# Turning float64 words into float32 on VectorE, with the intermediate word in a PSUM bank instead of in SBUF

## The chip, the cores and the metric

The kernel runs on one core of one Trainium2 chip. The metric is the device time of one execution in microseconds (us). A core has five engines with a queue of their own: TensorE (PE, with its weight loads as PEld), VectorE (DVE), ScalarE (ACT), GpSimd (POOL) and SyncE (SP, which issues the DMAs). Each works through its queue in order; semaphores hold an instruction back until what it needs is there. SBUF is the working memory, PSUM the eight banks into which TensorE writes.

## The reference

Three stages in a row: causal softmax attention, a gated block with a short causal convolution, and a block that mixes tokens with a sine and a cosine.

```python
# q, k, v: (4, 12, 448, 64) -> attention output x: (4, 448, 768)
scores = np.where(mask, -1e9, (1/8) * q @ k.T)
attn   = softmax(scores) @ v
# second block, weights 768 x 768, conv_w 5 x 768
gate = sigmoid(sum over t of conv_w[t] * x shifted by t)
x2   = (gate * (x @ w_val)) @ w_out
# third block, w_tok_r and w_tok_i 448 x 448
theta = x2 @ w_theta
y = w_tok_r @ (x2 * cos(theta)) + w_tok_i @ (x2 * sin(theta))
u = x2 + y
out = u + max(u @ w_ch, 0)
```

q, k and v arrive as float32. The seven weight arrays arrive as float64, so each number is two 32-bit words, a low one and a high one, and the kernel has to make float32 of them itself.

## The kernel before, in words

The first batch's attention (12 heads, one iteration of `attn_iter` each, in five pieces) runs alone; from then on `dense(b)` of one batch is interleaved with the attention of batch b+1, by the table `RATE`. `dense(b)` runs four stages of six column blocks of 128: x @ w_val with the gate (`hf`), w_out (`x2f`), theta with sine and cosine, the token mix (`ztr`, `tok`), and w_ch. Every matrix product is made with numbers that are split into a high and a low part, three matmuls for one. The tile tool, not the source, settles the final order on each engine: it reorders what the source asks for.

Conversion of weights: `load_w(n, g)` brings half a column block as 128 x 384 pairs of words into a tile `cv_raw` (48 of these; ring "wb" of 8 buffers, shared with `w_hl`). `stage_w` calls `to_f32` on it (L152 to L161), `split_w` has POOL make the high part (L104) and POOL or DVE the low part (L107, L110) in a tile `w_hl`, which L226 writes to DRAM for the later batches. `load_tok` does the same for eight 112 x 448 pieces of the token weights (`tok_bits`, into `tok_raw`), and `setup_conv` for 30 x 128 words of the convolution weights. That makes 57 calls of `to_f32`, all of them in the first 310 us of the execution.

`to_f32` has four steps, on views of the tile that take every second word: L152 (DVE) turns the low word into a number of 0 to 7; L155 (DVE) adds the sign of the high word to it; L158 (ACT) scales the high word; L159 (DVE) shifts it by three and joins both. L155 and L159 are the two with two tensor operands.

PSUM: `psum(tag)` hands out banks: two for the tag "mm" (matrix products), six for every other tag, all of them in one ring named "at". The scores `ps_s` (L320, L321, read by DVE at L322 and by ACT at L115), the transposes `ps_tr` (L283, L341, L394, L569, L610) and the attention output `ps_av` (L364, read by DVE at L424) all live in that ring of six.

Of the kernel before, what the change touches and what calls it, by code (L numbers as in the profile page):

```python
# [9 lines left out]
F32 = mybir.dt.float32  # L10
F32R = mybir.dt.float32r
I32 = mybir.dt.int32
U32 = mybir.dt.uint32
AF = mybir.ActivationFunctionType
ALU = mybir.AluOpType
# [33 lines left out]
def kernel(  # L49
# [14 lines left out]
    nc = tc.nc  # L64
# [34 lines left out]
    def psum(tag):  # L99
        at = "mm" if tag == "mm" else "at"  # L100
        return ps.tile([P, 512], F32, tag=at, name=f"ps_{tag}", bufs=2 if tag == "mm" else 6)
# [36 lines left out]
    def setup_conv():  # L138
        t = pool.tile([P, CV, 2], I32, tag="wb", name="cv_raw", bufs=8)
        nc.sync.dma_start(  # L140
            out=t[: KW * KC, 0:P, :].rearrange("p n two -> p (n two)"),
            in_=conv_w.rearrange("k (c n) -> (k c) n", n=2 * P),
        )
        c32 = pool.tile([P, S], F32, tag="tmp", name="c32")[:, 0:P]
        to_f32(c32[: KW * KC, :], t[: KW * KC, 0:P, :])
        pt = psum("tr")
        nc.tensor.transpose(pt[:, : KW * KC], c32[: KW * KC, :], ident[: KW * KC, : KW * KC])
        nc.vector.tensor_copy(cw.rearrange("p k c -> p (k c)"), pt[:, : KW * KC])

    def to_f32(dst, raw):  # L150
        hi, lo = raw[:, :, 1], raw[:, :, 0]
        nc.vector.tensor_scalar(  # L152
            out=lo, in0=lo.bitcast(U32), scalar1=2.0**-29, scalar2=7.0, op0=ALU.mult, op1=ALU.min
        )
        nc.vector.scalar_tensor_tensor(  # L155
            out=lo, in0=hi, scalar=-(2**31), in1=lo, op0=ALU.bitwise_and, op1=ALU.bitwise_or
        )
        nc.scalar.activation(hi.bitcast(F32), hi.bitcast(F32), AF.Abs, scale=2.0**-112)  # L158
        nc.vector.scalar_tensor_tensor(  # L159
            out=dst.bitcast(I32), in0=hi, scalar=3, in1=lo, op0=ALU.logical_shift_left, op1=ALU.bitwise_or  # L160
        )  # L161

    tok_raw = []
# [1 line left out]
    def load_tok(c):  # L165
        t = pool.tile([P, NZ * P], F32, tag=("zt_h", "zt_l")[c % 2], name="tok_raw")
        for a, w in enumerate((w_tok_r, w_tok_i)):
            r = pool.tile([P, S, 2], I32, tag="z", name="tok_bits", bufs=3)
            nc.sync.dma_start(
                out=r[:CP].rearrange("p n two -> p (n two)"), in_=w[c * CP : (c + 1) * CP, :]  # L170
            )
            to_f32(t[:CP, a * S : (a + 1) * S], r[:CP])
        tok_raw.append(t)
# [28 lines left out]
    def stage_w(n, g):  # L202
        if n < NW:
            to_f32(bits[n, g][:, :, 0], bits[n, g])
# [546 lines left out]
```

## Time and profile before

| | |
|---|---|
| median of 3 runs | 796.83 us (794.93 to 798.34) |
| the profiled execution, its own time | 796.42 us |
| its span, first to last instruction | 794.6 us |
| PE busy | 713.9 us (90%) |
| DVE busy | 503.7 us (63%) |
| ACT busy | 429.3 us (54%) |
| POOL busy | 314.4 us (40%) |
| TensorE's mean granted clock | 0.976 |

The shares are averages over stages that differ. The chain of waits is the chain of work that ended last, followed back from the end: what stands on it set the time, and what does not stand on it was covered by other work. A group's mean against its minimum or its median tells how much of its time was waiting inside the instruction.

### The profile page before, as it was taken

What the parts mean: (1) busy time and instruction counts of PE and PEld (TensorE: products, weight loads), DVE (VectorE), ACT (ScalarE), POOL (GpSimd) and SP (SyncE); (2) the same over time, 40 slices, a digit from 0 to 9 for tenths busy, and PEclk for the clock granted to TensorE, in tenths of its full rate; (3) what the DMA queues carried; (4) which work ended last, traced back from release to release, by engine and by line L of the source; (5) the groups of instructions that cost most, each with busy time, mean ns of one, the idle gap of its engine ahead of it and who ended that gap; (6) DMA issues with size and microseconds to landing.
All of it is one profiled execution on the core that took longest, in us unless ns stands there. A gap on an engine that the chain in (4) does not pass through costs nothing.

```text
span 794.6 us, 11969 instructions
## 1 busy us (share of the span) xinstructions
PE 713.9 (90%) x3989; PEld 603.9 (76%) x3989; DVE 503.7 (63%) x1131; ACT 429.3 (54%) x1004; POOL 314.4 (40%) x327
## 2 busy tenths in 40 slices
PE   6977897696879898999899899999899999999997
PEld 4555576575667787788788788788798797988996
DVE  4889989999997655643756644752766733115531
ACT  5888765546577643544777633544787522125401
POOL 0688795574553766332235610122133232201100
PEclk9999899899999999999989999999999999999999
DMA  9546359688765279678833159678814068774323
GB/s 234 118 118 187 104 129 323 139 256 208 222 122 144 44 232 254 184 201 216 172 78 84 43 166 210 171 188 199 178 45 103 14 144 231 216 221 128 94 67 84
DMA packets 145419, 124.63 MB, mean 157 GB/s; under 512 B 87855, under 2 KB 120397, under 8 KB 145357
## 3 DMA queue, kind: packets, MB, share of 16 engines
q1 hardware_dynamic: 145357, 123.86, 60.5%
q8 instruction: 32, 0.52, 0.3%
q14 instruction: 30, 0.25, 0.1%
HBM read 99.38 MB, written 24.44 MB: 156 GB/s over the span
## 4 chain that ended last, share of the span: by engine, by line
PE 52%; DVE 22%; DMA 9%; ACT 8%; POOL 4%; issue 3%; SPq 0%; ACTq 0%; DVEq 0%; POOLq 0%
PE ps_mm L488 28%; PE ps_mm L583 10%; DMA out_dram<-o 4%; PE ps_av L364 4%; PE ps_tr L341 3%; DVE cv_raw L155 3%; DVE ps_s L322 2%; DVE cv_raw L159 2%; PE ps_s L320 2%; DVE gate L450 2%; PE ps_s L321 2%; DVE qs L110 2%; DVE cv_raw L152 2%; ACT prob L115 2%; PE ps_tr L569 1%
## 5 line engine op out<-in xcount | busy, mean ns | idle before, releaser
L488 PE MATMUL ps_mm<-act_hi,w_hl 128*128 128x448 f32 x864 | 272.7, 377 | 15.0 <-POOL w_hl L104 5.4
L488 PEld LDWEIGHTS ps_mm<-act_hi,w_hl 128*128 128x128 f32 x864 | 164.3, 192 | 32.4 <-POOL w_hl L104 6.8
L488 PE MATMUL ps_mm<-act_lo,w_hl 128*128 128x448 f32 x432 | 159.9, 371 | 0.8 <-DVE act_lo L110 0.8
L115 ACT ACTIVATE prob<-ps_s,negm 112x112 f32<-112x112 f32 x192 | 95.1, 497 | 64.7 <-DVE negm L322 63.2
L322 DVE CUSTOM_DVE_ANT_0 ps_s<-ps_s,mask 112x112 f32<-112x112 f32 x192 | 85.6, 455 | 62.9 <-PE ps_s L321 52.0
L107 POOL TENSOR_TENSOR act_lo<-x2f,act_hi 128x448 fp32r<-128x448 f32 x36 | 43.6, 1210 | 128.6 <-ACT act_hi L502 63.0
L320 PE MATMUL ps_s<-kk,qs 128*112 128x256 f32 x192 | 71.2, 374 | 18.9 <-DVE qs L110 7.2
L488 PEld LDWEIGHTS ps_mm<-act_lo,w_hl 128*128 128x128 f32 x432 | 82.8, 192 | 6.3 <-DVE act_lo L110 1.2
L354 ACT COPY pt<-ps_tr 112x448 f32<-112x448 f32 (+2 forms) x120 | 51.4, 440 | 61.2 <-PE ps_tr L341 60.6
L341 PE MATMUL ps_tr<-ident,prob 112*112 112x112 f32 x480 | 78.7, 269 | 6.2 <-ACT prob L115 3.2
L488 PE MATMUL ps_mm<-x_hi,w_hl 128*128 128x448 f32 x264 | 79.4, 369 | 2.1 <-DVE hf L526 1.7
L341 PEld LDWEIGHTS ps_tr<-ident,prob 112*112 112x112 f32 x480 | 56.4, 137 | 20.3 <-ACT prob L115 7.8
L583 PE MATMUL ps_mm<-wtok_h,zt_h 128*128 128x448 f32 x168 | 64.5, 384 | 5.6 <-ACT zt_h L574 5.6
L583 PE MATMUL ps_mm<-wtok_h,zt_l 128*128 128x448 f32 x168 | 63.5, 378 | 0.1
L583 PE MATMUL ps_mm<-wtok_l,zt_h 128*128 128x448 f32 x168 | 62.3, 371 | 0.0
L321 PE MATMUL ps_s<-klo,qs 128*112 128x256 f32 x192 | 60.4, 326 | 1.8 <-DVE klo L110 1.8
L446 POOL TENSOR_TENSOR gate<-gate,tp 128x448 f32<-128x448 f32 x48 | 58.8, 1225 | 2.3
L364 PE MATMUL ps_av<-pt,v_raw 112*64 112x448 f32 (+3 forms) x384 | 58.7, 419 | 0.4 <-ACT prob L115 0.4
L559 POOL TENSOR_TENSOR z<-z,x2f 128x448 f32<-128x448 f32 x18 | 21.3, 1184 | 87.7 <-ACT z L556 87.6
L107 POOL TENSOR_TENSOR x_lo<-xf,x_hi 128x448 fp32r<-128x448 f32 x23 | 29.2, 1268 | 67.1 <-ACT x_hi L429 66.7
L488 PEld LDWEIGHTS ps_mm<-x_hi,w_hl 128*128 128x128 f32 x264 | 49.4, 188 | 8.3 <-DVE hf L526 3.4
L320 PEld LDWEIGHTS ps_s<-kk,qs 128*112 128x112 f32 x192 | 34.8, 183 | 27.3 <-DVE qs L110 5.0
(101 smaller groups left out, 1377.1 us busy)
## 6 DMA issues: line engine op xcount, KB each, us to landing
w_hl<-scratch SPq DMA_DIRECT2D x144, 384.0 KB, 3.9
scratch<-w_hl SPq DMA_DIRECT2D x44, 384.0 KB, 3.9
q_raw<-in_q_dram SPq DMA_DIRECT2D x48, 112.0 KB, 3.5
k_raw<-in_k_dram SPq DMA_DIRECT2D x48, 112.0 KB, 3.6
v_raw<-in_v_dram SPq DMA_DIRECT2D x24, 224.0 KB, 3.6
out_dram<-o SPq DMA_DIRECT2D x24, 224.0 KB, 3.3
cv_raw<-in_moe_w_val_dram SPq DMA_DIRECT2D x12, 384.0 KB, 4.9
cv_raw<-in_moe_w_out_dram SPq DMA_DIRECT2D x12, 384.0 KB, 6.5
```

Of the source, the lines that this page charges most:

```text
L107: nc.gpsimd.tensor_tensor(out=dst, in0=src, in1=f32(hi), op=ALU.subtract)
L115: exps.append(nc.scalar.activation(*args, **kw))
L155: nc.vector.scalar_tensor_tensor(out=lo, in0=hi, scalar=-(2**31), in1=lo, op0=ALU.bitwise_and, op1=ALU.bitwise_or)
L320: nc.tensor.matmul(pt[:CP, :nn], lhsT=qs[:, cs], rhs=kk[:, :nn], start=True, stop=False)
L321: nc.tensor.matmul(pt[:CP, :nn], lhsT=qs[:, cs], rhs=klo[:, :nn], start=False, stop=True)
L322: ttr = nc.vector.tensor_tensor_reduce(out=pt[:CP, :n], in0=pt[:CP, :n], in1=mask[:, S - n : S], scale=-1.0 / math.sqrt(D), scalar=3.0e38, ...
L341: nc.tensor.transpose(pt[:CP, off : off + CP], prob[i, c][:, kc * CP : (kc + 1) * CP], ident[:CP, :CP])
L354: nc.scalar.copy(t, src)
L364: nc.tensor.matmul(av[g][j * D : (j + 1) * D, kc * CP : S], lhsT=tv[:, j, kc, :], rhs=pT.pop((2 * g + j, kc)), start=kc == 0, stop=kc == N ...
L446: nc.gpsimd.tensor_tensor(out=gt, in0=gt, in1=tp, op=ALU.add)
L488: nc.tensor.matmul(pt[:, :S], lhsT=a[:, kc % KH, :], rhs=x, start=kc == 0 and m == 0, stop=kc == KC - 1 and m == 2,)
L583: nc.tensor.matmul(pt[:, :S], lhsT=a[:, m, :], rhs=w[:, m, :], start=m == 0 and n == 0, stop=m == NZ - 1 and n == 2,)
```

## The change

`to_f32` takes one more tile, from the PSUM ring "at", and L152 and L155 write the intermediate word there. ACT's step then writes into the low word of the raw tile, no longer in place of the high word, so it needs no more than that L152 has read the low word.

```diff
     def to_f32(dst, raw):
         hi, lo = raw[:, :, 1], raw[:, :, 0]
+        low = psum("cv")[: raw.shape[0], : raw.shape[1]].bitcast(I32)
         nc.vector.tensor_scalar(
-            out=lo, in0=lo.bitcast(U32), scalar1=2.0**-29, scalar2=7.0, op0=ALU.mult, op1=ALU.min
+            out=low, in0=lo.bitcast(U32), scalar1=2.0**-29, scalar2=7.0, op0=ALU.mult, op1=ALU.min
         )
         nc.vector.scalar_tensor_tensor(
-            out=lo, in0=hi, scalar=-(2**31), in1=lo, op0=ALU.bitwise_and, op1=ALU.bitwise_or
+            out=low, in0=hi, scalar=-(2**31), in1=low, op0=ALU.bitwise_and, op1=ALU.bitwise_or
         )
-        nc.scalar.activation(hi.bitcast(F32), hi.bitcast(F32), AF.Abs, scale=2.0**-112)
+        nc.scalar.activation(lo.bitcast(F32), hi.bitcast(F32), AF.Abs, scale=2.0**-112)
         nc.vector.scalar_tensor_tensor(
-            out=dst.bitcast(I32), in0=hi, scalar=3, in1=lo, op0=ALU.logical_shift_left, op1=ALU.bitwise_or
+            out=dst.bitcast(I32), in0=lo, scalar=3, in1=low, op0=ALU.logical_shift_left, op1=ALU.bitwise_or
         )
```

The line that is added moves every later line by one: L152, L155, L158 and L159 of before are L153, L156, L159 and L160 of after. The number of instructions stays the same on each engine but ACT (818 instead of 814), yet the tile tool, which orders by what each step needs, puts them in another order all through the first part of the program. Two places on VectorE show how. The numbers behind names tell tiles of the same name apart.

The first is on VectorE in the attention of the first batch, at the second `cv_raw` tile. Before:

```order
L152 TENSOR_SCALAR cv_raw_256<-cv_raw_256 128x384
L159 SCALAR_TENSOR_TENSOR cv_raw_185<-cv_raw_185 128x384
L155 SCALAR_TENSOR_TENSOR cv_raw_256<-cv_raw_256 128x384
L322 ISA ps_s_365,negm_244<-ps_s_365,mask_67 112x112
L322 ISA negm_244 112x1
L424 TENSOR_TENSOR xf0_72<-ps_av_320,rb_318 128x448
L322 ISA ps_s_377,negm_244<-ps_s_377,mask_67 112x224
L322 ISA negm_244 112x1
L159 SCALAR_TENSOR_TENSOR cv_raw_256<-cv_raw_256 128x384
```

And now:

```order
L160 SCALAR_TENSOR_TENSOR cv_raw_186<-cv_raw_186,ps_cv_272 128x384
L323 ISA ps_s_309,negm_245<-ps_s_309,mask_67 112x448
L323 ISA negm_245 112x1
L153 TENSOR_SCALAR ps_cv_350<-cv_raw_257 128x384
L156 SCALAR_TENSOR_TENSOR ps_cv_350<-cv_raw_257,ps_cv_350 128x384
L160 SCALAR_TENSOR_TENSOR cv_raw_257<-cv_raw_257,ps_cv_350 128x384
L425 TENSOR_TENSOR xf0_72<-ps_av_322,rb_320 128x448
L323 ISA ps_s_368,negm_245<-ps_s_368,mask_67 112x112
```

The three DVE steps of one conversion, which stood apart, now follow each other directly, and the step of the attention output (L424, now L425) comes after all three.

The second place is on VectorE where the token weights are converted, at the start of `dense(0)`. Before:

```order
L152 TENSOR_SCALAR tok_bits_1361<-tok_bits_1361 112x448
L152 TENSOR_SCALAR tok_bits_1367<-tok_bits_1367 112x448
L110 TENSOR_TENSOR klo1_75<-ps_tr_1316,kk_1329 64x448
L155 SCALAR_TENSOR_TENSOR tok_bits_1361<-tok_bits_1361 112x448
L155 SCALAR_TENSOR_TENSOR tok_bits_1367<-tok_bits_1367 112x448
L110 TENSOR_TENSOR act_lo_1357<-hf_1354,act_hi_1356 128x448
L322 ISA ps_s_1438,negm_1336<-ps_s_1438,mask_67 112x112
L322 ISA negm_1336 112x1
L322 ISA ps_s_1470,negm_1336<-ps_s_1470,mask_67 112x224
L322 ISA negm_1336 112x1
```

And now:

```order
L153 TENSOR_SCALAR ps_cv_1379<-tok_bits_1377 112x448
L153 TENSOR_SCALAR ps_cv_1389<-cv_raw_1142 128x384
L153 TENSOR_SCALAR ps_cv_1409<-cv_raw_1144 128x384
L156 SCALAR_TENSOR_TENSOR ps_cv_1372<-tok_bits_1370,ps_cv_1372 112x448
L110 TENSOR_TENSOR act_lo_1366<-hf_1363,act_hi_1365 128x448
L156 SCALAR_TENSOR_TENSOR ps_cv_1379<-tok_bits_1377,ps_cv_1379 112x448
L156 SCALAR_TENSOR_TENSOR ps_cv_1389<-cv_raw_1142,ps_cv_1389 128x384
L156 SCALAR_TENSOR_TENSOR ps_cv_1409<-cv_raw_1144,ps_cv_1409 128x384
L160 SCALAR_TENSOR_TENSOR tok_raw_1369<-tok_bits_1370,ps_cv_1372 112x448
L527 SCALAR_TENSOR_TENSOR hf_1425<-gate_715,ps_mm_1384 128x448
```

Four `ps_cv` tiles (1372, 1379, 1389, 1409) are in use here at once, out of a ring of six; the scores of the next head (L322, now L323), which stood among the conversions, come later. On SP the loads of the token weights and of w_out move the same way, some steps earlier among the writes of `w_hl`.

## Rows read from the trace of the kernel before

**Rows 1.** The page: busy time, share of the span, instructions of each engine.

```profile
PE 713.9 (90%) x3989; PEld 603.9 (76%) x3989; DVE 503.7 (63%) x1131; ACT 429.3 (54%) x1004; POOL 314.4 (40%) x327
```

**Rows 2.** Busy time by stretch: start:end, length, each engine, TensorE clock, DMA share, GB/s.

```profile
50.00:105.00 55.00, 45.43 (x277) 31.71 (x278) 49.42 (x128) 44.31 (x128) 46.95 (x52) 0.94 0.48 135
105.00:150.00 45.00, 33.69 (x180) 27.17 (x180) 43.95 (x83) 22.60 (x52) 32.08 (x32) 0.98 0.81 234
150.00:200.00 50.00, 41.38 (x206) 33.19 (x206) 49.55 (x97) 28.86 (x71) 27.75 (x29) 0.91 0.78 203
200.00:250.00 50.00, 40.34 (x231) 33.95 (x230) 45.95 (x91) 30.45 (x64) 24.26 (x25) 0.97 0.71 179
...
310.00:400.00 90.00, 85.38 (x494) 73.88 (x493) 46.83 (x114) 48.91 (x115) 23.79 (x22) 0.99 0.79 204
```

**Rows 3.** The chain that ended last, shares by line, from 50 to 250 us.

```profile
by line: DVE cv_raw L155 8.3%; DVE cv_raw L159 7.7%; issue 6.4%; DVE cv_raw L152 5.0%; DMA cv_raw<-in_moe_w_ch_dram 4.5%; DVE ps_s L322 4.5%; DMA cv_raw<-in_moe_w_out_dram 3.9%; PE ps_mm L488 3.5%; PE ps_av L364 2.9%; DVE tok_raw L159 2.8%;
```

**Rows 4.** The same chain from 105 to 200 us.

```profile
by line: DMA cv_raw<-in_moe_w_out_dram 8.2%; DVE cv_raw L155 8.2%; DVE cv_raw L159 7.7%; issue 6.6%; DVE tok_raw L159 6.0%; DVE tok_bits L152 5.6%; DVE cv_raw L152 5.2%; DVE ps_s L322 5.1%; DVE tok_bits L155 3.7%; PE ps_mm L488 3.7%; DMA k_
```

**Rows 5.** DVE groups by form: xcount | busy us, mean ns | idle before, releasers.

```profile
L155 DVE SCALAR_TENSOR_TENSOR cv_raw<-cv_raw 128x384 int32<-128x384 int32 x48 | 40.6, 847 | 0.4
L159 DVE SCALAR_TENSOR_TENSOR cv_raw<-cv_raw 128x384 int32<-128x384 int32 x48 | 36.8, 767 | 2.9 <-ACT cv_raw L158 2.7
L152 DVE TENSOR_SCALAR cv_raw<-cv_raw 128x384 int32<-128x384 uint32 x48 | 24.4, 508 | 5.4 <-DMA cv_raw<-in_moe_w_ch_dram 4.6 <-DMA cv_raw<-in_moe_w_out_dram 0.8
L159 DVE SCALAR_TENSOR_TENSOR tok_raw<-tok_bits 112x448 int32<-112x448 int32 x8 | 9.0, 1126 | 0.0
L152 DVE TENSOR_SCALAR tok_bits<-tok_bits 112x448 int32<-112x448 uint32 x8 | 7.0, 890 | 0.0
L155 DVE SCALAR_TENSOR_TENSOR tok_bits<-tok_bits 112x448 int32<-112x448 int32 x8 | 6.8, 862 | 0.0
```

**Rows 6.** The same instructions by tile: duration ns min/median/max, first and last start.

```profile
L152 DVE TENSOR_SCALAR cv_raw<-cv_raw x49: 218/358/1300, 12.1 to 301.3; 128x384 int32<-128x384 uint32 x48, 30x128 int32<-30x128 uint32 x1
L155 DVE SCALAR_TENSOR_TENSOR cv_raw<-cv_raw x49: 280/560/1514, 12.3 to 301.7; 128x384 int32<-128x384 int32 x48, 30x128 int32<-30x128 int32 x1
L159 DVE SCALAR_TENSOR_TENSOR cv_raw<-cv_raw x48: 498/560/1493, 25.7 to 303.7; 128x384 int32<-128x384 int32 x48
```

**Rows 7.** DVE in order of time, 94.8 to 99.2 us: start, length, instruction.

```profile
94.91 0.52 DVE L152 TENSOR_SCALAR cv_raw<-cv_raw 128x384 int32<-128x384 uint32 x1
...
95.88 0.97 DVE L155 SCALAR_TENSOR_TENSOR cv_raw<-cv_raw 128x384 int32<-128x384 int32 x1
97.53 1.46 DVE L159 SCALAR_TENSOR_TENSOR cv_raw<-cv_raw 128x384 int32<-128x384 int32 x1 [0.68 <-ACT cv_raw L158]
```

**Rows 8.** POOL in the same stretch.

```profile
95.30 1.14 POOL L446 TENSOR_TENSOR gate<-gate,tp 128x448 f32<-128x448 f32 x1
...
97.44 1.14 POOL L446 TENSOR_TENSOR gate<-gate,tp 128x448 f32<-128x448 f32 x1
```

**Rows 9.** DVE groups that read PSUM and SBUF, the first two also writing PSUM.

```profile
L322 DVE CUSTOM_DVE_ANT_0 ps_s<-ps_s,mask 112x448 f32<-112x448 f32 x48 | 30.2, 629 | 10.0 <-PE ps_s L321 9.7
L322 DVE CUSTOM_DVE_ANT_0 ps_s<-ps_s,mask 112x336 f32<-112x336 f32 x48 | 24.8, 516 | 23.7 <-PE ps_s L321 13.6 <-ACT pt L354 8.9 <-ACT o L614 1.0
L526 DVE SCALAR_TENSOR_TENSOR hf<-gate,ps_mm 128x448 f32<-128x448 f32 x24 | 14.6, 616 | 30.4 <-PE ps_mm L488 28.8 <-PE ps_mm L467 1.3 <-issue 0.3
```

**Rows 10.** Waits of PE, 0 to 310 us: waiter <- releaser: us in total, times, longest.

```profile
PE ps_s L320 <- DVE pt L352: 3.9, 1, 3.9
PE ps_s L320 <- ACT prob L115: 2.4, 2, 1.6
PE ps_s L320 <- ACT pt L354: 1.0, 2, 0.8
```

**Rows 11.** Waits of DVE and ACT in that stretch, round the third step.

```profile
ACT cv_raw L158 <- DVE cv_raw L155: 24.0, 21, 2.8
...
DVE cv_raw L159 <- ACT cv_raw L158: 2.7, 6, 0.7
```

## The prediction

> **What bounds the kernel now.** I read the page's busy times first, then the busy time by stretch, then the chain, and last the conversion steps one by one. Over the whole span PE is the busiest engine, at 90% [rows 1], and after 310 us it sets the pace alone: 85.4 us busy of 90 [rows 2]. The four stretches before it are another matter. From 105 to 200 us DVE is busy 43.95 of 45 and 49.55 of 50 us, while PE has 33.7 and 41.4; from 50 to 105 and from 200 to 250 us DVE has 49.4 of 55 and 45.95 of 50 [rows 2]. So for 200 us, from 50 to 250, DVE is the engine that is nearly full. The chain says the same: from 50 to 250 us its largest items are L155 with 8.3% and L159 with 7.7%, both steps of the conversion, with L152 at 5.0% and the last step of the token weights at 2.8% [rows 3]. Those steps are what the change touches.
>
> Now the steps themselves. L155 and L159 have a median of 560 ns on 128x384, but maxima of 1514 and 1493 [rows 6], and means of 847 and 767 [rows 5]. Nothing is inside them but the same 384 columns, so the rest is waiting within the instruction. What for can be seen at one place: L155 starts at 95.88 and takes 0.97 us, while POOL's L446 runs from 95.30 to 96.44; L159 starts at 97.53 and takes 1.46 us, while the next L446 runs from 97.44 to 98.58 [rows 7, 8]. Each DVE step ends 0.41 us after the POOL step. DVE got going only when POOL had finished. POOL's L446 reads and writes SBUF alone, as L155 and L159 do. The DVE steps with one tensor operand in PSUM show no such excess: L526 has a mean of 616 ns over 24 on 448 columns, and L322, which also writes PSUM, 629 [rows 9].
>
> **The change part by part.** All durations are of the profiled execution, 796.4 us of its own time (span 794.6), 0.4 us under the median of the runs.
>
> *The two long steps.* Their second operand comes from PSUM. Undisturbed price: L322 with 336 and 448 columns takes 516 and 629 ns [rows 9], so 516 + 48 x 113/112 = 564 ns for 384, the same as today's median of 560 [rows 6]. I take 560, and 616 ns for 448 columns, from L526. Against the means [rows 5], DVE gets back 48 x (847 - 560) = 13.8 us in L155, 48 x (767 - 560) = 9.9 in L159, and on the token weights 8 x (862 - 616) = 2.0 and 8 x (1126 - 616) = 4.1. Together 29.8 us of busy time. Above, the bound is all of it; below, it is nothing, if the wait for POOL doesn't hang on the operands.
>
> [...]
>
> *L152.* It has one source, and its output moves to PSUM. Today the median is 358 ns for 384 columns and 218 ns for the 30x128 call [rows 6]: 0.55 ns a column, where L322 needs 113 ns for 112 [rows 9]. A step with PSUM in it may well go at the latter, which is 564 ns (lower bound 358, if its speed stays). I take 564. The mean before is 508, waits included [rows 5], so 48 x (564 - 508) = 2.7 us are lost; on the token weights 629 replaces 890, and 8 x 261 = 2.1 are won. Over all, nothing.
>
> *What of it lies on the chain.* From 50 to 250 us the shares are 16.6 us of L155, 15.4 of L159, 10.0 of L152 and 5.6 of the token L159 [rows 3]; the token L152 and L155 have 5.6% and 3.7% of 95 us, 5.3 and 3.5 [rows 4]. [...] Each scaled by what goes: 16.6 x 287/847 = 5.6; 15.4 x 207/767 = 4.2; 5.6 x 510/1126 = 2.5; 3.5 x 246/862 = 1.0; L152 10.0 x -56/508 = -1.1; 5.3 x 261/890 = 1.6. Sum 13.8 us. The stretches before 50 and after 250 us I put at nothing: there PE and the loads cover it.
>
> *What is late next.* Loads of w_out and w_ch are on the chain already, with 3.9% and 4.5% [rows 3], and the DMA engines' share is 0.81 and 0.78 from 105 to 200 us [rows 2]. A tenth of the gain, 1.4 us, I leave to them.
>
> *The banks.* Each of 57 calls takes a tile of the ring of six that scores, transposes and attention outputs share. It is held from L152 to the end of L159, 94.91 to 98.99 us in the one place, 4.1 us [rows 7]. PE waits today for readers of older tiles of that ring for 3.9 + 2.4 + 1.0 = 7.3 us up to 310 us [rows 10]. Two batches of attention take 24 x 7 + 12 x 4 = 216 tiles there, by the code; 57 more are 26%, so 1.9 us more. I take 2.0; the upper bound is in the second rival. Behind a score that waits stands all of PE's queue, the matrix products too.
>
> *ACT, and order.* L158 no longer waits for L155, which it did for 24.0 us; but DVE waited for L158 only 2.7 us [rows 11], so little is to be had. Where L153, L156 and L160 follow each other directly, DVE may wait for ACT instead, some 0.1 us each. Zero for both, 2.7 either way. POOL's share of the conversion (L104, L107) comes sooner; DVE's waiting isn't on it. The loads on SP stand a few places earlier and are as many: zero. The other instructions are the same in another order, which I can't price and leave to the range.
>
> **Sum:** 13.8 - 1.4 - 2.0 = 10.4 us off 796.4, so **786 us**. The range of this case is 775 to 792: 775 if L152 keeps its 358 ns and more of the 29.8 us than 13.8 arrives at the end, 792 if half of it is lost.
>
> **The rivals.**
> *The gain is swallowed.* DVE is emptier and the same moment comes no sooner, since the loads of w_out and w_ch set it. For: their shares on the chain [rows 3] and the DMA share of 0.81 [rows 2]. Against: DVE is 98% busy there, and the loads take ring buffers that the conversions give back. If of 13.8 us the 9 or so that fall after 105 us go, 13.8 - 9 - 2 = 2.8 stay: 794.
> *The banks turn it round (slower).* The mechanism is PE at L320 and L341, waiting for a bank that a conversion holds while DVE's queue is full; in the order of after four `ps_cv` tiles are in use at once beside six banks. 57 x 4.1 us are 234 us of one bank, 39 us of all six. If half of that becomes idle time of PE, the time is 796.4 - 12.4 + 19.5 = 803.5. It decides from 12.4 us on, 0.22 us a conversion. Against: PE's waits of that kind are 7.3 us today [rows 10], and the attention of the second batch has slack in its table.
> *The change doesn't do what it says.* The wait for POOL stays in L155 and L159, and only L152 gets slower: 48 x (564 - 358) = 9.9 us busy, half of it on the chain, plus 2 for the banks: 803; with L152's own waits gone, 798.5. Against it stand the even means of L526 and L322 [rows 9].
>
> **How the numbers follow.** What a measurement of this kernel can tell from no change is about 0.5%, 4 us: 792.8 and 800.8. The forecast gets 0.66, all of it faster. The swallowed gain gets 0.17, all within. The banks get 0.11, slower. The last rival gets 0.06, half within and half slower. That makes 0.66 faster, 0.20 same, 0.14 slower. The range, 775 to 800, leaves out the slower cases (0.14) and a tail below.
>
> **What would show it.** In the profile after: the means of the two long steps (L156 and L160 there) at 0.56 to 0.60 us on 384 columns and maxima far under 1.5; L153 at about 0.56; DVE from 105 to 200 us under 93% busy, or that work done sooner; the last conversion ending some 10 us before 304 us [rows 6]; waits of PE on `ps_cv` readers (L160) no more than a few us. It is wrong if the long steps still reach 1.5 us, if PE waits over 12 us for banks, or if DVE idles while DMA waits grow by what DVE lost.

## The result, and the profile after

The change takes 787.87 us, median of 4 runs (783.01 to 791.92), against 795.88 us of the kernel before, also 4 runs. The ratio is 0.989, with a 95% interval of 0.986 to 0.992: about 8 us faster, 1.1%. The profiled execution is the fastest of the four: 783.01 us, span 781.2. Its busy times, on the page:

```profile
PE 714.5 (91%) x3989; PEld 607.4 (78%) x3989; DVE 475.6 (61%) x1131; ACT 432.6 (55%) x1008; POOL 295.9 (38%) x327
```

Against [rows 1], DVE has 28.1 us less to do (503.7 to 475.6), POOL 18.5 us less, ACT 3.3 us more, and PE the same. By stretch, in the columns of [rows 2]:

```profile
50.00:105.00 55.00, 49.44 (x303) 37.25 (x302) 44.77 (x124) 44.65 (x128) 47.78 (x56) 0.96 0.51 137
105.00:150.00 45.00, 36.60 (x195) 29.67 (x194) 44.02 (x97) 25.85 (x61) 26.17 (x30) 0.92 0.89 265
150.00:200.00 50.00, 38.55 (x186) 29.98 (x186) 42.63 (x98) 31.71 (x70) 24.47 (x29) 0.85 0.82 210
200.00:250.00 50.00, 45.34 (x247) 37.72 (x244) 39.48 (x90) 37.88 (x80) 23.73 (x28) 0.91 0.55 146
```

From 105 to 150 us DVE is as full as before, 44.0 of 45 us. It is no longer full from 150 to 250 us: 42.6 of 50 and 39.5 of 50 us, where it had 49.55 and 45.95. PE has more work done from 50 to 150 us (303 and 195 matmuls, before 277 and 180) and from 200 to 250 (247, before 231), but less from 150 to 200 (186, before 206).

Something else moved there. TensorE's granted clock was 0.92, 0.85 and 0.91 of full speed in the three stretches from 105 to 250 us, where it had been 0.98, 0.91 and 0.97 [rows 2]. In these two traces it stands at full speed or at half of it (0.50 from 242.8 to 249.4 us here, and from 76.9 to 83.6 us before); up to 310 us it stood at half for 44.4 us in all, before for 27.3. One of these spells, from 194.9 us, began while PE had run nothing since 190.5. The change is faster in spite of this, and PE's busy time stayed where it was (714.5, before 713.9); what the lower clock cost it, no run separates.

The conversion steps, first by form with their means, then by tile with minimum, median, maximum and the first and last start:

```profile
L153 DVE TENSOR_SCALAR ps_cv<-cv_raw 128x384 int32<-128x384 uint32 x48 | 26.9, 565 | 4.8 <-DMA cv_raw<-in_moe_w_theta_dram 1.9 <-ACT prob L115 1.4 <-DMA cv_raw<-in_moe_w_ch_dram 1.2
L156 DVE SCALAR_TENSOR_TENSOR ps_cv<-cv_raw,ps_cv 128x384 int32<-128x384 int32 x48 | 26.6, 558 | 0.6
...
L160 DVE SCALAR_TENSOR_TENSOR cv_raw<-cv_raw,ps_cv 128x384 int32<-128x384 int32 x48 | 26.1, 546 | 2.2 <-ACT cv_raw L159 1.5
...
L156 DVE SCALAR_TENSOR_TENSOR ps_cv<-tok_bits,ps_cv 112x448 int32<-112x448 int32 x8 | 5.0, 626 | 0.0
...
L160 DVE SCALAR_TENSOR_TENSOR tok_raw<-tok_bits,ps_cv 112x448 int32<-112x448 int32 x8 | 4.9, 611 | 0.0
```

```profile
L153 DVE TENSOR_SCALAR ps_cv<-cv_raw x49: 312/553/600, 11.8 to 286.6; 128x384 int32<-128x384 uint32 x48, 30x128 int32<-30x128 uint32 x1
L156 DVE SCALAR_TENSOR_TENSOR ps_cv<-cv_raw,ps_cv x49: 282/555/595, 12.1 to 287.8; 128x384 int32<-128x384 int32 x48, 30x128 int32<-30x128 int32 x1
...
L160 DVE SCALAR_TENSOR_TENSOR cv_raw<-cv_raw,ps_cv x48: 493/547/581, 25.1 to 288.8; 128x384 int32<-128x384 int32 x48
```

These lines answer to [rows 5] and [rows 6]. The long steps have means of 558 and 546 ns, where they had 847 and 767, and no maximum over 595, where there were 1514 and 1493. The first step went from a mean of 508 to 565, from a median of 358 to 553. The last conversion starts its last step at 288.8 us, before at 303.7: 14.9 us sooner, and the span is 13.4 us shorter. So all that was won in this execution was won before that moment, and nothing after it. The chain from 50 to 250 us, for [rows 3]:

```profile
by line: PE ps_mm L489 9.9%; issue 5.9%; PE ps_mm L584 3.4%; PE ps_av L365 2.9%; DVE ps_cv L153 2.4%; DMA cv_raw<-in_moe_w_out_dram 2.2%; DMA rb<-rows 2.0%; DVE cv_raw L160 1.7%; DVE ps_cv L156 1.7%; DVE gate L451 1.6%; DVE ps_s L323 1.4%; 
```

Where the three steps of the weights held 21% of that chain, they hold 5.8% now, and the matrix products (L489) come first.

PE's waits for the new tiles in the ring of six, and the one line that is left of a score's waits for the older readers, 0 to 310 us:

```profile
PE ps_tr L342 <- DVE tok_raw L160: 2.2, 1, 2.2
PE ps_tr L342 <- DVE cv_raw L160: 2.2, 2, 1.2
PE ps_s L321 <- ACT prob L115: 1.8, 3, 0.7
...
PE ps_s L321 <- DVE tok_raw L160: 1.6, 1, 1.6
...
PE ps_s L321 <- DVE cv_raw L160: 1.2, 1, 1.2
```

A transpose or a score that waits for L160 waits for the bank that the conversion held: 2.2 + 2.2 + 1.6 + 1.2 = 7.2 us, waits which the kernel before cannot have. But the waits of a score for the older readers went down: of the 7.3 us in [rows 10] only the 1.8 for L115 are left. By these lines together PE waits 9.0 us for banks of the ring, before 7.3.

### The profile page after: what moved, and what is told of

Its sections match the earlier page's. It is cut to its first block, busy times and chain, and to the rows that moved or that the text cites. A ratio compares the mean times of both kernels' runs of the same rounds, so it can differ in the third digit from the quotient of the medians.

```text
span 781.2 us, 12060 instructions
## 1 busy us (share of the span) xinstructions
PE 714.5 (91%) x3989; PEld 607.4 (78%) x3989; DVE 475.6 (61%) x1131; ACT 432.6 (55%) x1008; POOL 295.9 (38%) x327
## 4 chain that ended last, share of the span: by engine, by line
PE 53%; DVE 10%; DMA 8%; ACT 7%; issue 2%; POOL 1%; SPq 0%; ACTq 0%; DVEq 0%; POOLq 0%
PE ps_mm L489 31%; PE ps_mm L584 11%; DMA out_dram<-o 5%; PE ps_av L365 3%; PE ps_tr L342 2%; DVE gate L451 2%; PE ps_s L321 2%; PE ps_s L322 2%; DMA scratch<-w_hl 2%; ACT L557 1%; PE ps_tr L570 1%; DVE qs L110 1%; ACT prob L115 1%; DMA rb<-rows 1%; ACT L115 1%
## 5 line engine op out<-in xcount | busy, mean ns | idle before, releaser
L489 PE MATMUL ps_mm<-act_hi,w_hl 128*128 128x448 f32 x864 | 268.8, 373 | 3.4 <-DVE w_hl L110 1.7
L489 PEld LDWEIGHTS ps_mm<-act_hi,w_hl 128*128 128x128 f32 x864 | 162.6, 190 | 18.2 <-DVE w_hl L110 2.0
L489 PE MATMUL ps_mm<-act_lo,w_hl 128*128 128x448 f32 x432 | 158.9, 369 | 0.0
L323 DVE CUSTOM_DVE_ANT_0 ps_s<-ps_s,mask 112x112 f32<-112x112 f32 x192 | 86.1, 454 | 67.7 <-PE ps_s L322 55.3
L115 ACT ACTIVATE prob<-ps_s,negm 112x112 f32<-112x112 f32 x192 | 95.3, 498 | 57.4 <-DVE negm L323 54.8
L489 PEld LDWEIGHTS ps_mm<-act_lo,w_hl 128*128 128x128 f32 x432 | 82.1, 191 | 5.1
L489 PE MATMUL ps_mm<-x_hi,w_hl 128*128 128x448 f32 x264 | 81.5, 378 | 2.2 <-DVE hf L527 1.2
L321 PE MATMUL ps_s<-kk,qs 128*112 128x256 f32 x192 | 72.8, 383 | 11.0 <-ACT kk L308 2.9
L322 PE MATMUL ps_s<-klo,qs 128*112 128x256 f32 x192 | 62.8, 336 | 4.1 <-DVE klo L110 4.1
L365 PE MATMUL ps_av<-pt,v_raw 112*64 112x224 f32 (+3 forms) x384 | 58.9, 428 | 0.3 <-DVE klo L110 0.2
L447 POOL TENSOR_TENSOR gate<-gate,tp 128x448 f32<-128x448 f32 x48 | 56.5, 1177 | 2.7
L489 PEld LDWEIGHTS ps_mm<-x_hi,w_hl 128*128 128x128 f32 x264 | 50.7, 193 | 8.6 <-DVE hf L527 2.9
L365 PEld LDWEIGHTS ps_av<-pt,v_raw 112*64 112x64 f32 x384 | 28.2, 143 | 29.9 <-issue 17.4
```

Source lines behind the costliest of these rows:

```text
L115: exps.append(nc.scalar.activation(*args, **kw))
L321: nc.tensor.matmul(pt[:CP, :nn], lhsT=qs[:, cs], rhs=kk[:, :nn], start=True, stop=False)
L322: nc.tensor.matmul(pt[:CP, :nn], lhsT=qs[:, cs], rhs=klo[:, :nn], start=False, stop=True)
L323: ttr = nc.vector.tensor_tensor_reduce(out=pt[:CP, :n], in0=pt[:CP, :n], in1=mask[:, S - n : S], scale=-1.0 / math.sqrt(D), scalar=3.0e38, ...
L365: nc.tensor.matmul(av[g][j * D : (j + 1) * D, kc * CP : S], lhsT=tv[:, j, kc, :], rhs=pT.pop((2 * g + j, kc)), start=kc == 0, stop=kc == N ...
L447: nc.gpsimd.tensor_tensor(out=gt, in0=gt, in1=tp, op=ALU.add)
```

## The experiments

Three theories stood to be told apart. **Port:** the long steps waited for POOL because both their tensor operands lay in SBUF, and the gain is that time. **Early start:** ACT's step no longer waits for the first long step, and the gain is the shorter conversion. **Order:** the tile tool ordered everything anew, and the gain is that of another order. A fourth question was the price of the banks. Each kernel was timed beside the kernel before on the same chip; its median there was between 796.8 and 798.4 us in the three sets of runs, so ratios are what to compare. A diff stands against the change, unless the text says that it is the kernel before; `...` in one stands for code that stays. Where no interval stands, there was a single run.

### Which engine the long steps waited for

The kernel before, with four of five taps of the convolution left out on POOL:

```diff
-            for t in range(1, KW):
+            for t in range(1, 1):
                 nc.gpsimd.tensor_scalar(
```

> The kernel before with four of five taps of the convolution left out where GpSimd computes them (12 of 24 blocks): GpSimd loses 96 instructions, 94 us, most of them before 105 us. Port theory: the two long steps lose their waits there, a mean under 0.62 us up to 105 us where it was 0.93 and 0.76, and keep them later, where GpSimd splits weights. Rival (the waits come from memory layout or the loads, not from GpSimd): the means stay as they were.

The two long steps up to 105 us, by form, in the kernel before:

```profile
L155 DVE SCALAR_TENSOR_TENSOR cv_raw<-cv_raw 128x384 int32<-128x384 int32 x12 | 11.3, 945 | 0.1
...
L159 DVE SCALAR_TENSOR_TENSOR cv_raw<-cv_raw 128x384 int32<-128x384 int32 x12 | 8.8, 736 | 2.0 <-ACT cv_raw L158 1.9
```

and with the taps left out:

```profile
L159 DVE SCALAR_TENSOR_TENSOR cv_raw<-cv_raw 128x384 int32<-128x384 int32 x12 | 6.9, 572 | 1.9 <-ACT cv_raw L158 1.9
L155 DVE SCALAR_TENSOR_TENSOR cv_raw<-cv_raw 128x384 int32<-128x384 int32 x12 | 6.7, 555 | 0.1
```

The DVE instructions are the same ones on the same data; with POOL's taps left out they take 555 and 572 ns. The waits were for POOL. The trace of the kernel before, gone through instruction by instruction, says the same: of its 98 long steps in `cv_raw` and the convolution weights, the 35 during which no POOL instruction ran took 561 ns at most, and the long ones, up to 1514 ns, all had one beside them. Whether this hangs on both operands lying in SBUF, the next two experiments test one step at a time. That a single operand there is not always safe, the first step shows: L152 has one tensor operand, and it too reaches 1300 ns [rows 6]. Of its 49 the 18 without a POOL instruction beside them took 361 ns at most, and the four longest ended 0.22 to 0.23 us after one. In PSUM it loses this wait (no L153 over 600 ns), but also the 358 ns of its median: L153 has 553.

The time, 799.5 us in one run, did not fall with it; DVE waited for weight loads instead:

```profile
L152 DVE TENSOR_SCALAR cv_raw<-cv_raw 128x384 int32<-128x384 uint32 x48 | 23.0, 478 | 15.6 <-DMA cv_raw<-in_moe_w_out_dram 8.6 <-DMA cv_raw<-in_moe_w_ch_dram 5.4 <-DMA cv_raw<-in_moe_w_theta_dram 1.4
```

That is 15.4 us before L152 for three of the loads, against 5.4 us for two in [rows 5]. DVE's busy time was 20.8 us less there (503.7 to 482.9), and the one run shows no gain from it.

### One long step at a time

The last step alone with an operand in PSUM: L152 writes SBUF, L155 reads SBUF alone and writes PSUM, ACT works in place of the high word as before.

```diff
-            out=low, in0=lo.bitcast(U32), ...
+            out=lo, in0=lo.bitcast(U32), ...
-            out=low, in0=hi, scalar=-(2**31), in1=low, ...
+            out=low, in0=hi, scalar=-(2**31), in1=lo, ...
-        nc.scalar.activation(lo.bitcast(F32), hi.bitcast(F32), ...)
+        nc.scalar.activation(hi.bitcast(F32), hi.bitcast(F32), ...)
-            out=dst.bitcast(I32), in0=lo, scalar=3, in1=low, ...
+            out=dst.bitcast(I32), in0=hi, scalar=3, in1=low, ...
```

> Only the last step has an operand in PSUM: the first step and the first long step read SBUF alone (the long step writes PSUM), ScalarE in place as before. Port theory: the first long step stays at 0.80 to 0.90 us, the last at 0.55, the first step between 0.36 and 0.55; some 15 us of VectorE time come back instead of 28, and the time is half way, 790 to 793 us. Early-start rival: 795 to 797 us, as ScalarE starts late. Order rival: not tied to this, 783 to 800 us.

The first long step alone: L152 writes PSUM, the long step reads it and writes SBUF, the last step reads SBUF alone, ACT in place.

```diff
-            out=low, in0=hi, scalar=-(2**31), in1=low, ...
+            out=lo, in0=hi, scalar=-(2**31), in1=low, ...
-        nc.scalar.activation(lo.bitcast(F32), hi.bitcast(F32), ...)
+        nc.scalar.activation(hi.bitcast(F32), hi.bitcast(F32), ...)
-            out=dst.bitcast(I32), in0=lo, scalar=3, in1=low, ...
+            out=dst.bitcast(I32), in0=hi, scalar=3, in1=lo, ...
```

> Only the first long step has an operand in PSUM; it writes SBUF, and the last step reads SBUF alone, ScalarE in place as before. Port theory: the first long step 0.55 to 0.57 us, the last one 0.72 to 0.82 as before, the first step 0.565; some 14 us of VectorE time come back, 790 to 794 us. Early-start rival: 795 to 797 us.

The steps by form, last step alone:

```profile
L156 DVE SCALAR_TENSOR_TENSOR ps_cv<-cv_raw 128x384 int32<-128x384 int32 x48 | 38.7, 809 | 0.9 <-ACT prob L115 0.4
...
L153 DVE TENSOR_SCALAR cv_raw<-cv_raw 128x384 int32<-128x384 uint32 x48 | 26.5, 557 | 14.2 <-DMA cv_raw<-in_moe_w_ch_dram 6.5 <-DMA cv_raw<-in_moe_w_theta_dram 3.9 <-DMA cv_raw<-in_moe_w_out_dram 2.8
L160 DVE SCALAR_TENSOR_TENSOR cv_raw<-cv_raw,ps_cv 128x384 int32<-128x384 int32 x48 | 26.0, 547 | 10.6 <-ACT cv_raw L159 10.3
```

and first long step alone:

```profile
L160 DVE SCALAR_TENSOR_TENSOR cv_raw<-cv_raw 128x384 int32<-128x384 int32 x48 | 32.6, 684 | 6.4 <-ACT cv_raw L159 6.4
...
L153 DVE TENSOR_SCALAR ps_cv<-cv_raw 128x384 int32<-128x384 uint32 x48 | 27.0, 564 | 2.9 <-ACT prob L115 1.4 <-DMA cv_raw<-in_moe_w_out_dram 1.2 <-DMA cv_raw<-in_moe_w_theta_dram 0.3
...
L156 DVE SCALAR_TENSOR_TENSOR cv_raw<-cv_raw,ps_cv 128x384 int32<-128x384 int32 x48 | 26.0, 548 | 0.5
```

As durations go, the port theory holds to the step: whichever step has one operand outside SBUF takes 547 or 548 ns, the one with two inside takes 809 or 684. The output in PSUM doesn't spare a step the wait (809 with PSUM out), the second operand does. As times go it fails: with the last step alone 807.16 us, a ratio of 1.014 (1.010 to 1.017), slower; with the first long step alone 788.6 us, 0.990 (0.987 to 0.994), the whole gain of the change for 21.5 us of DVE's busy time (503.7 to 482.2) in place of 28.1. DVE's time is not the only price. In the slow one DVE waits 13.2 us before L153 for loads. From the trace's starts and ends, its 57 conversions last 11.6 us on the mean from the start of the first step to the end of the last, 9.1 of them to the end of the first long step, where the kernel before needs 6.6 and 2.9. That raw tiles held for longer delay the next loads would fit, but it is only argued; why the first long step stands so late there was not tried.

### ScalarE's early start

The change with ACT in place of the high word, so that it waits for the first long step again:

```diff
-        nc.scalar.activation(lo.bitcast(F32), hi.bitcast(F32), ...)
+        nc.scalar.activation(hi.bitcast(F32), hi.bitcast(F32), ...)
-            out=dst.bitcast(I32), in0=lo, scalar=3, in1=low, ...
+            out=dst.bitcast(I32), in0=hi, scalar=3, in1=low, ...
```

> The word of low bits and sign in PSUM as in the change, but ScalarE works in place of the high word as before, so it has to wait for the first long step again. Port theory (the long steps waited for GpSimd because both operands were in SBUF): both long steps stay at 0.55 to 0.57 us on 384 columns, the time stays at 785 to 791 us. Early-start rival (the gain comes from ScalarE starting one step earlier): most of the 8 us goes, 793 to 797 us. Order rival (the gain is that of another order of instructions): no relation to the durations, anywhere from 783 to 800 us.

It took 799.79 us, 1.003 (1.000 to 1.006): the gain was gone, and a little more than the early-start rival had (793 to 797 us), though the long steps are as short as in the change:

```profile
L153 DVE TENSOR_SCALAR ps_cv<-cv_raw 128x384 int32<-128x384 uint32 x48 | 26.8, 563 | 16.2 <-DMA cv_raw<-in_moe_w_ch_dram 7.4 <-DMA cv_raw<-in_moe_w_out_dram 3.2 <-ACT prob L115 3.2
L156 DVE SCALAR_TENSOR_TENSOR ps_cv<-cv_raw,ps_cv 128x384 int32<-128x384 int32 x48 | 26.8, 564 | 0.6
...
L160 DVE SCALAR_TENSOR_TENSOR cv_raw<-cv_raw,ps_cv 128x384 int32<-128x384 int32 x48 | 26.0, 548 | 8.1 <-ACT cv_raw L159 8.1
```

What is new stands behind the bars: DVE idles 8.1 us before L160 for ACT, where the change has 1.5 there, and 16.2 us before L153, 12.7 of them for loads of weights (the row's 10.6, and 2.1 for w_theta), where the change has 4.8 and 3.1. To see how much of this is order, both versions were run again with `A_TILES` one piece later, (11, 15, 23, 29, 35, 41, 47, 53) for (10, 14, 22, 28, 34, 40, 46, 52): the same work, ordered anew.

> The change, with each of the first eight conversions of weights asked for one piece of attention later in the source: the same work, in another order by the tile tool. A control on what order alone is worth. If little: 785 to 791 us. If the order is worth as much as the parts of the change: below 782 or above 794 us.

> The same shift for the experiment with ScalarE in place (799.8 us). If its loss is due to the late start of ScalarE: 796 to 803 us again. If it was an unlucky order: 786 to 793 us, as the change.

The change so shifted took 789.12 us, 0.991 (0.988 to 0.994), as before the shift. The version with ACT in place took 794.08 us, 0.997 (0.995 to 1.000), between the two expectations. Its runs are spread from 786.8 to 797.1 us; the fastest is as fast as the fastest of the shifted change (786.4). So order alone moves a version by 0.002 to 0.006 in ratio, up to 4.5 us, and between the early and the late start lie 0.006 in one order and 0.0135 in the other: 5 to 11 us.

A late start is not dear by itself, though. The version with the first long step alone starts ScalarE late too, and by the traces its conversions last as long, 5.4 us on the mean from the start of the first step to the end of the last, against 5.3 in the version with ACT in place (4.3 in the change). Yet it has the whole gain, 0.990 against 1.003, with 3.1 us more of DVE's busy time (482.2 against 479.1). What differs is how long the bank is held: to the end of the first long step, 2.7 us on the mean, in place of 5.3. That speaks for the hold of the bank, and against the age of the raw tile, as what a late start costs here; the tile tool ordered these versions anew as well, so another order is not excluded, but it would have to be worth 0.0123, twice what the shift moved.

### The price of the banks

The kernel before with five banks in the ring (`6` to `5` in `psum`):

> The kernel before with five banks in place of six in the ring of scores, transposes and attention outputs, over the whole program, nothing else. By the small price of a bank that the prediction took (2 us for a quarter more tiles): 797 to 801 us. By the rival that banks are dear: over 804 us, with TensorE waiting over 15 us more for readers of older tiles.

820.08 us, 1.029 (1.025 to 1.033): one bank of six is worth 23 us. The expectation that banks are dear was right as to time, but not in where to see it: PE's waits in the trace for readers of older tiles did not grow by 15 us. The longest in total stand before the transposes of L569:

```profile
PE ps_tr L569 <- ACT pt L354: 6.1, 3, 3.0
...
PE ps_tr L569 <- DVE pt L352: 3.6, 1, 3.6
```

Where the rest of the 23 us went was not settled; it may be the order, which the tool makes anew for five banks. A part shows in TensorE itself, by the page and by stretch:

```profile
PE 731.0 (90%) x3989; PEld 614.8 (75%) x3989; DVE 508.1 (62%) x1131; ACT 430.8 (53%) x1006; POOL 314.2 (39%) x327
```

```profile
150.00:200.00 50.00, 41.97 (x199) 34.24 (x199) 48.26 (x98) 27.61 (x70) 30.39 (x31) 0.83 0.73 192
200.00:250.00 50.00, 38.87 (x185) 31.41 (x186) 45.57 (x85) 31.27 (x63) 24.76 (x24) 0.83 0.64 174
```

The same 3989 matmuls keep PE busy for 731.0 us, before 713.9, and its granted clock is 0.83 in both stretches, where it was 0.91 and 0.97 [rows 2]. What half speed does to a matmul the trace of the kernel before shows: of its L583, the 11 that ran wholly in a spell of half speed have a median of 575 ns, the 489 wholly outside one 367. So some of what the bank cost is likely to be matmuls at the lower clock. What made it fall was not tried.

Then the change with a bank for the word alone and five for the rest:

```diff
-        at = "mm" if tag == "mm" else "at"
-        return ps.tile([P, 512], F32, tag=at, name=f"ps_{tag}", bufs=2 if tag == "mm" else 6)
+        at = tag if tag in ("mm", "cv") else "at"
+        return ps.tile([P, 512], F32, tag=at, name=f"ps_{tag}", bufs={"mm": 2, "cv": 1}.get(tag, 5))
```

> The change, but the word has one of the six banks for itself and scores, transposes and attention outputs keep five. The kernel before with five banks took 820 us, 22 more than before. Bank theory (the change gives back part of its gain because conversions hold banks of the shared ring for 4.3 us each): sharing is cheaper than a bank of one's own, so 800 to 808 us, that is 820 less the 12 to 20 us that VectorE gets back. Port theory with banks at no price: as the change, 786 to 792 us.

804.52 us, 1.010 (1.007 to 1.013): as the bank theory had it. With five banks on both sides the change's step is from 1.029 to 1.010, 15 us, more than the 8.6 us (0.011 of 797) with six banks shared. And the same with ACT in place:

> ScalarE in place of the high word, as in the experiment that lost the gain (799.8 us), and the word in a bank of its own, as in the one that took 804.5 us with ScalarE's early start. If the early start paid by giving banks back to attention sooner (a hold of 4.3 us a conversion instead of 5.3), it is worth little with a bank apart: 803 to 808 us. If it paid because the conversion itself is over sooner: 812 to 818 us. If neither, but the order the tile tool made: anything between.

810.9 us, 1.018 (1.016 to 1.020): between the two, the early start is worth 0.0085, 6.8 us, with a bank apart. So the early start is worth something even where the conversion holds no bank that the attention wants. Why, is not shown: the raw tile is done sooner, and its next load can start sooner; but with one bank for the word each conversion also stands behind the last step of the one before, and by the traces one lasts 3.5 us in place of 3.0.

### The price of VectorE's time

The change with its first long step written twice, which gives the same word. The 44 per cent of its expectation are the 41.1 us of the two long steps that lay on the chain [rows 3, 4], of 93.2 us busy [rows 5]:

> The change with the first long step done twice, to the same result: 57 more VectorE instructions of 0.56 to 0.62 us, 32 us, about what the change took from VectorE, without any wait for GpSimd, and a bank held 0.6 us longer. Port theory, with 44 per cent of such time on the chain: 14 us more than the change, 799 to 804 us. If VectorE's time counts in full: 815 to 820. If the gain was not VectorE's time: 786 to 791 us.

800.48 us, 1.004 (1.002 to 1.006), 0.0147 more than the change: 11.7 us. The second time adds

```profile
L159 DVE SCALAR_TENSOR_TENSOR ps_cv<-cv_raw,ps_cv 128x384 int32<-128x384 int32 x48 | 27.0, 565 | 0.3
...
L159 DVE SCALAR_TENSOR_TENSOR ps_cv<-tok_bits,ps_cv 112x448 int32<-112x448 int32 x8 | 5.0, 620 | 0.0
```

27.0 + 5.0 us, and 0.3 for the convolution weights. So a microsecond of VectorE that is added to these conversions costs 11.7 / 32.3 = 0.36 us at the end; some of that is the bank, held 0.6 us longer. Taken away, it is not always worth as much: 20.8 us less brought nothing where POOL's taps were left out, 24.6 us less nothing with ACT in place.

### A version that is faster

The first step on ScalarE in all conversions, and in every second one. With the factor 0.93 the largest word comes to 7.44, which makes 7 whether it is rounded or cut, so the `min` is not needed; the three low bits can come out a little differently:

```diff
-        nc.vector.tensor_scalar(
-            out=low, in0=lo.bitcast(U32), scalar1=2.0**-29, scalar2=7.0, op0=ALU.mult, op1=ALU.min
-        )
+        nc.scalar.activation(low, lo.bitcast(U32), AF.Copy, scale=2.0**-29 * 0.93)
```

> The first step of a conversion is made on ScalarE in place of VectorE (scale by a little less than 2^-29 and round, so the last of 24 bits can differ), into the same PSUM tile; the rest as in the change. VectorE loses another 32 us of work in the first 300 us, ScalarE takes as much. If VectorE still sets the pace there: 774 to 783 us. If the pace has gone over to loads and TensorE: 785 to 790 us. If ScalarE becomes the one waited for: over 790 us.

> Every second conversion has its first step on ScalarE, the others on VectorE as in the change. With all on ScalarE the time was 784 us and VectorE waited 24 us for those steps. If a balance of both is better: 778 to 783 us. If the pace is no longer set by either: 783 to 788 us, as the change or the other version.

783.86 us, 0.984 (0.981 to 0.988), and 784.43 us, 0.985 (0.983 to 0.987): the fastest of the study, 12 us under the kernel before, the same for both. They are some 4 us under the change, but the intervals overlap, so this is likely and not shown. VectorE loses 25.6 us more of busy time (475.6 to 450.0), but stands and waits for ACT:

```profile
L154 DVE SCALAR_TENSOR_TENSOR ps_cv<-cv_raw,ps_cv 128x384 int32<-128x384 int32 x48 | 26.9, 563 | 24.2 <-ACT ps_cv L153 24.0
```

24.0 us before the first long step. At 0.36 the 25.6 us would have been 9 us; some 4 came.

## Why the prediction was right, point by point

The time was forecast as 786 us and is 787.87; the parts were not all as forecast.

- **The long steps.** Right: 560 ns were taken and 558 and 546 measured (616 and then 626 and 611 on the token weights), no long step exceeds 595 ns on 384 columns any more, and leaving out POOL's work shows that it was POOL. One reading was too strong: a step of 560 ns that ends 0.41 us after POOL's [rows 7, 8] had done an estimated 0.15 us of its work before POOL finished. That an operand in PSUM would cost the long steps nothing of its own held too: the trace has means of 546 and 558 ns with one, against a median of 560 without [rows 6].
- **L152.** Right: 564 was taken, 565 measured. Its 358 ns were lost, and its waits with them.
- **What lies on the chain.** About right: 0.44 of the two steps' time was reckoned to count, the doubled step gives 0.36. For the 28.1 us that DVE lost this is 10 us, where the sum had 13.8 less 1.4. The last conversion's last step starts 14.9 us sooner, where some 10 were forecast, in the fastest of the four runs.
- **ACT's early start.** The step "Zero for both, 2.7 either way" was too low: it was priced by DVE's wait for L158, 2.7 us [rows 11], and what a late ScalarE does to the hold of the bank was left out. Three pairs give 4.7, 6.8 and 10.8 us between an early and a late start. These are prices inside the change, where the bank waits with ScalarE; the version with the first long step alone starts late and loses nothing.
- **The banks.** By PE's waits about right: 2.0 us more were taken, and the lines of L160 and of the readers in [rows 10] went from 7.3 to 9.0 us in all. The sign "no more than a few us" for L160 alone was missed, at 7.2. By what is left over it depends on the reading. If the early start is a gain of its own, 8.6 = 10 + (5 to 11) - X, and X, what banks, order and the lower clock took together, is 6 to 12 us; then two misses, one each way, hid each other, and the time came out by luck. If the early start pays by the shorter hold of the bank, it stands in the bank's price already, and 8.6 = 10 - 1.4. The version with the first long step alone speaks for the second: its 21.5 us of DVE at 0.36 are 7.7 us, and its 0.0096 are 7.7 us, with nothing left for a late start. It does not decide it, since 0.36 is not a constant.
- **The loads.** A tenth was left to them. In the change DVE's wait for loads of weights fell from 5.4 us to 3.1, so there is no sign that they swallowed anything; in three versions without a gain it rose, to 12.7 (ACT in place), 13.2 (last step alone) and 15.4 us (taps left out).

What stays open: which of the two readings holds, how much of the time the order and TensorE's lower clock took, and why the version with the last step alone is slower than the kernel before.

## What to carry to other kernels

A VectorE step whose mean is far above its median, as 847 ns against 560 here, may be waiting inside the instruction; when it ends soon after a GpSimd instruction (here 0.41 us) and both its operands lie in SBUF, try a second operand in PSUM: here it took the wait away (means of 558 and 546 ns) at no other cost to the two long steps. A step with one operand that ran fast in SBUF, as L152 did with a median of 358 ns, paid for the move here: 553. The bank must come from somewhere: look at how long each step holds it, and shorten that hold (start the parallel step early, give the bank back at the first chance); here the version that gave it back after the first long step had the whole gain with a quarter less of DVE's saving. And when a sum comes out right, test its zero terms as well as its large ones: here the start of ScalarE, put at zero, moved versions of the change by 4.7 to 10.8 us, where the whole gain is 8.6.

## What the hardware showed beyond what was expected

POOL gained too: its busy time fell from 314.4 to 295.9 us with the same 327 instructions. By the traces, POOL's L104 into `w_hl` took 728 ns on the mean before when it overlapped a step of a conversion (32 of 44) and 541 when not; after the change it is 606 (21 of 44) and 569. So POOL was slowed as well where the two met. A VectorE step with a single tensor operand waited for POOL as well: L152, 358 ns at the median and 361 at most with no POOL instruction beside it, reached 1300 [rows 6]. One bank of six was worth 23 us to a kernel whose traced waits for banks were 7.3 us up to 310 us [rows 10].
